# Linear attention and a two-layer FFN in float32: the second stage's up product by Strassen's scheme, with weight sums made early and streamed

## The chip, the cores and the metric

The kernel runs on one core of a Trainium2 chip. The metric is the device time in microseconds (us) of one execution. Three executions of the kernel before took 1128.74, 1130.81 and 1132.51 us; the median, 1130.81 us, is the number to compare with. The profile describes one execution, with the span from its first to its last instruction.

## The reference

Inputs are float32: q, k, v of 8 batches x 8 heads x 576 tokens x 64, a feature matrix w_phi (64 x 128), the FFN weights w_in (512 x 2048) and w_out (2048 x 512), and a slope alpha for each of the 2048 hidden features.

```python
def phi(x):
    proj = np.einsum('bhsd,df->bhsf', x, w_phi)
    proj = proj - np.max(np.abs(proj), axis=-1, keepdims=True)
    return np.concatenate([np.exp(proj), np.exp(-proj)], axis=-1)
q_p, k_p = (phi(q), phi(k))
kv = np.einsum('bhsf,bhsd->bhfd', k_p, v)
z = np.sum(k_p, axis=2)
num = np.einsum('bhsf,bhfd->bhsd', q_p, kv)
den = np.einsum('bhsf,bhf->bhs', q_p, z)[..., None] + 1e-06
x = (num / den)            # 4608 tokens x 512 after a transpose
h = x @ w_in
g = np.maximum(h, 0.0) + alpha * np.minimum(h, 0.0)
return g @ w_out
```

## The kernel before

The whole kernel is one pass with the output transposed (512 features x 4608 tokens). Attention goes by 32 pairs of heads (`attention_units(i)`); the FFN goes by nine chunks of 512 tokens and by sixteen hidden tiles of 128 features. A full-precision product is made of three matmuls on halves: each operand is split into a rounded high half and the remainder, and high x high, low x high and high x low are added in PSUM (`gemm1` for the up product, `gemm2` for the down product). One hidden tile of one chunk takes 4 x 3 matmuls up and 4 x 3 down, each 128 x 128 x 512.

**Two stages.** The first NF1 = 5 hidden tiles make the first stage: their weights stay in SBUF, and their chunks (`ffn1_units`) are woven into attention as soon as the tokens of a chunk are there. Their partial outputs go to `part_d` in DRAM. The other NF2 = 11 tiles make the second stage, after attention: `up2`, `glu2` and `down2` for each chunk and tile, with the weights kept in SBUF, the sum in four PSUM banks (`po`), and at a chunk's end the addition of `part_d` (L745) and the store. The last two first-stage chunks run between the first tiles of the second stage.

**The order.** For everything up to the turn to the second stage the order is written out by hand: each piece of work is put in `todo` with a due time in steps of one attention pair, and the list is sorted; PE, SP, DVE and ACT keep that order. `turn_over` at T2 = 35.4 frees attention's memory and starts the loads of the second stage's weights. In the second stage (`pass2`) only PE's order is fixed; a planner orders the other engines by its own simulation. POOL is never fixed.

**Weights.** They come as 64-bit floats. Each block of 128 x 256 is decoded by `decode_load` (SP, L177), `decode_scale` (ACT, L186), `decode_split` (DVE, L194 to L197), `decode_add` (POOL, L202), `decode_high` (ACT, L137), `decode_low` (POOL, L141) and `decode_store` (SP, L222). There are 20 blocks for the first stage, two to a pair step from the start, and 44 for the second, one every W2D = 0.70 pair steps from W2A = 12.5 on; so some are decoded after the turn. They pass through raw buffers (RW_BUFS = 4), whose store to `w_d` has to end before the buffer takes the next load. WT holds the offsets of a block's steps, from load at -0.70 to store at +0.90.

**Per tile.** `act_g` makes the leaky activation: two ACT reads of PSUM (L251, L252), a join on DVE (L256), the high half on ACT (L137) and the remainder on DVE (L141).

**Lines.** L141 is the helper `low`, a subtraction on the engine that it is given; L137 is a cast on ACT. L335 and L336 subtract a row's largest absolute value on DVE; L358 to L365 (`k_sum`) sum features for z; L487 divides by the denominator on POOL. L527 to L529 are `gemm1`, L534 to L538 `gemm2`. L582 copies a first-stage result from PSUM on ACT. L693 loads a chunk, L728 a partial output, L749 stores an output.

## Time and profile before

| what | value |
|---|---|
| median of three executions | 1130.81 us (1128.74 to 1132.51) |
| the profiled execution, first to last instruction | 1128.8 us |
| its own time beside the span | not listed apart; the shortest execution, 1128.74 us, is as long as the span |
| mean granted TensorE clock | 1.000 |
| attention and seven first-stage chunks | 0 to about 515 us |
| two last first-stage chunks with chunk 0 | about 520 to 600 us |
| second stage alone | from about 600 us on |
| HBM read, written | 93.92 MB, 38.42 MB |

Engines are PE (TensorE matmuls), PEld (its weight loads), DVE, ACT, POOL and SP (which issues most DMAs). A row of a group gives the line, engine and operation, the tiles, the shape and the count, then busy time and mean length (ns) of one, then the idle time before them with what ended it. A row of a table by stage gives the stretch, its length, the busy time of PE, PEld, DVE, ACT and POOL with counts, the granted clock, the share of DMA and GB/s. A row in order of time gives start, length, engine, line and operation. A row of one line's instructions gives shortest/median/longest length in ns.

The page's rows over forty slices of the span:

```profile
DVE  7888958797788777846872332424233423343323
ACT  4777665666666765665553342333333333333331
POOL 1245332332414142253541000000000000000000
```

### The profile page before, as it was taken

What the parts mean: (1) busy time and instruction counts of PE and PEld (TensorE: products, weight loads), DVE (VectorE), ACT (ScalarE), POOL (GpSimd) and SP (SyncE); (2) the same over time, 40 slices, a digit from 0 to 9 for tenths busy, and PEclk for the clock granted to TensorE, in tenths of its full rate; (3) what the DMA queues carried; (4) which work ended last, traced back from release to release, by engine and by line L of the source; (5) the groups of instructions that cost most, each with busy time, mean ns of one, the idle gap of its engine ahead of it and who ended that gap; (6) DMA issues with size and microseconds to landing.
All of it is one profiled execution on the core that took longest, in us unless ns stands there. A gap on an engine that the chain in (4) does not pass through costs nothing.

```text
span 1128.8 us, 18394 instructions
## 1 busy us (share of the span) xinstructions
PE 1114.8 (99%) x7246; PEld 868.3 (77%) x7246; DVE 636.9 (56%) x983; ACT 559.5 (50%) x1148; POOL 212.3 (19%) x217
## 2 busy tenths in 40 slices
PE   8999999999999999999999999999999999999998
PEld 6666777777777777677788888888888888888886
DVE  7888958797788777846872332424233423343323
ACT  4777665666666765665553342333333333333331
POOL 1245332332414142253541000000000000000000
PEclk9999999999999999999999999999999999999999
DMA  5467264546546364466627030303030302020011
GB/s 180 154 185 223 74 202 151 172 155 199 162 155 201 101 212 165 140 211 206 227 81 254 33 106 1 112 1 112 1 112 1 112 1 98 15 93 20 12 64 38
DMA packets 74389, 133.68 MB, mean 118 GB/s; under 512 B 14656, under 2 KB 25024, under 8 KB 73664
## 3 DMA queue, kind: packets, MB, share of 16 engines
q1 hardware_dynamic: 72000, 122.48, 33.7%
q0 software_dynamic: 2016, 9.96, 2.6%
q8 instruction: 57, 0.93, 0.3%
q14 instruction: 28, 0.23, 0.1%
q10 hardware_dynamic: 288, 0.07, 0.0%
HBM read 93.92 MB, written 38.42 MB: 117 GB/s over the span
## 4 chain that ended last, share of the span: by engine, by line
PE 90%; DVE 6%; DMA 2%; ACT 1%; issue 1%; SPq 0%; DVEq 0%; ACTq 0%
PE h L527 11%; PE h L529 11%; PE h L528 11%; PE po L534 8%; PE po L538 8%; PE po L536 8%; PE kv L372 5%; PE pj L331 5%; PE n L437 5%; PE o L534 4%; PE o L538 3%; PE o L536 3%; PE d L455 2%; PE qt L418 2%; DVE m L335 1%; PE kv L389 1%
## 5 line engine op out<-in xcount | busy, mean ns | idle before, releaser
L256 DVE SCALAR_TENSOR_TENSOR g<-r,aln,g 128x512 f32<-128x512 f32 x144 | 111.4, 774 | 312.1 <-ACT g L252 311.6
L251 ACT ACTIVATE r<-h 128x512 f32<-128x512 f32 x143 | 85.9, 601 | 276.3 <-PE h L529 276.1
L141 DVE TENSOR_TENSOR gl<-g,gh 128x512 fp32r<-128x512 f32 x144 | 104.3, 726 | 84.8 <-ACT gh L137 84.6
L137 ACT CAST gh<-g 128x512 fp32r<-128x512 f32 x144 | 90.0, 625 | 97.6 <-DVE g L256 97.5
L252 ACT ACTIVATE g<-h 128x512 f32<-128x512 f32 x144 | 85.8, 596 | 9.8 <-DVE r L249 6.4
L335 DVE TENSOR_REDUCE m<-pj 128x8 f32<-128x1024 f32 (+1 forms) x66 | 78.2, 1184 | 13.8 <-PE pj L331 13.7
L534 PE MATMUL po<-gh,wd 128*128 128x512 f32 x216 | 84.3, 391 | 0.2 <-ACT gh L137 0.2
L536 PE MATMUL po<-gh,wd 128*128 128x512 f32 x216 | 84.3, 390 | 0.0
L538 PE MATMUL po<-gl,wd 128*128 128x512 f32 x216 | 83.9, 390 | 0.0
L202 POOL TENSOR_TENSOR aw<-ew,aw 128x256 f32<-128x256 f32 x64 | 57.5, 899 | 127.5 <-DVE ew L197 126.9
L336 DVE TENSOR_TENSOR t<-pj,m 128x1024 f32<-128x1024 f32 (+1 forms) x66 | 78.7, 1192 | 2.4
L331 PEld LDWEIGHTS pj<-w_sb,raw 64*128 64x128 f32 x1024 | 63.5, 190 | 18.2 <-issue 11.7
L331 PE MATMUL pj<-w_sb,raw 64*128 64x128 f32 x1024 | 72.7, 281 | 4.1 <-DVE t L336 2.5
L534 PE MATMUL o<-gh,w 128*128 128x512 f32 x180 | 76.0, 422 | 0.4 <-ACT gh L137 0.2
L527 PE MATMUL h<-xh,w 128*128 128x512 f32 x180 | 76.0, 422 | 0.0
L487 POOL TENSOR_TENSOR s<-s,rr 128x576 f32<-128x576 f32 x32 | 47.8, 1492 | 142.0 <-DMA rr<-rec_d 107.9
L428 ACT ACTIVATE qf<-qt 128x512 f32<-128x512 f32 x128 | 68.4, 614 | 6.3 <-PE qt L418 6.3
L538 PE MATMUL o<-gl,w 128*128 128x512 f32 x180 | 71.0, 395 | 0.2 <-DVE gl L141 0.2
L534 PE MATMUL po<-gh,w 128*128 128x512 f32 x180 | 70.2, 390 | 0.7 <-ACT gh L137 0.7
L529 PE MATMUL h<-xl,w 128*128 128x512 f32 x180 | 70.7, 393 | 0.0
L536 PE MATMUL o<-gh,w 128*128 128x512 f32 x180 | 70.6, 392 | 0.0
L528 PE MATMUL h<-xh,w 128*128 128x512 f32 x180 | 70.5, 392 | 0.0
(110 smaller groups left out, 2407.7 us busy)
## 6 DMA issues: line engine op xcount, KB each, us to landing
xr<-x_d SPq DMA_DIRECT2D x18, 1024.0 KB
raw<-kq_dram SPq DMA_DIRECT2D x31, 576.0 KB
v<-v_dram SPq DMA_DIRECT2D x32, 320.0 KB
w_d<-raww SPq DMA_DIRECT2D x38, 256.0 KB
rr<-rec_d SPq DMA_DIRECT2D x64, 144.0 KB
x_d<-s SPq DMA_DIRECT2D x32, 288.0 KB
part_d<-os SPq DMA_DIRECT2D x36, 256.0 KB
pt<-part_d SPq DMA_DIRECT2D x9, 1024.0 KB
```

What stands on the lines that cost most here:

```text
L137: return act.copy(dst, src)
L141: return eng.tensor_tensor(dst, src, f(hi), op=ALU.subtract)
L251: act.activation(st["r"], ps, AF.Relu, scale=-1.0)
L256: dve.scalar_tensor_tensor(g, st["r"], aln[:, ff : ff + 1], g, op0=ALU.mult, op1=ALU.add)
L331: pe.matmul(dst[h, j], lhsT=c["raw"][hs, ts], rhs=w_sb[hs], start=True, stop=True)
L335: dve.tensor_reduce(m, src, axis=AX.X, op=ALU.max, apply_absolute_value=True)
L527: pe.matmul(ps, lhsT=wt[0][:, ws], rhs=xh, start=n == 0, stop=False)
L528: pe.matmul(ps, lhsT=wt[1][:, ws], rhs=xh, start=False, stop=False)
L529: pe.matmul(ps, lhsT=wt[0][:, ws], rhs=xl, start=False, stop=n == NK - 1)
L534: pe.matmul(ps, lhsT=wt[2][:, ws], rhs=gh, start=first, stop=False)
L536: pe.matmul(ps, lhsT=wt[3][:, ws], rhs=gh, start=False, stop=False)
L538: pe.matmul(ps, lhsT=wt[2][:, ws], rhs=gl, start=False, stop=last)
```

## The change

The number of first-stage tiles goes from 5 to 4, so the second stage has 12. They are grouped in NU = 6 units of two tiles. Chunk 0 is computed as before. Chunks 1 to 8 are taken as four pairs, and the up product of a unit with a pair of chunks is made as a 2 x 2 block product (two tiles x two halves of the 512 inputs x two chunks) with seven block products in place of eight, in the Strassen-Winograd form. A block product is 2 x 3 matmuls.

- **Weights.** The four weight sums of each unit are made while the weights are decoded (`sum_of`: a sum or difference on POOL, the high half on ACT, the remainder on POOL, a store on SP) and kept in DRAM (`u_d`) with the four plain blocks. Second-stage blocks are decoded every 0.46 pair steps from 10.6 on, so that all are through before the turn. For each pair of chunks, each unit's seven blocks are loaded by SP into one of two buffers (`load_up`). The down weights stay in SBUF.
- **Inputs.** `prepare` loads half the inputs of two chunks, makes four sums on POOL, and splits seven blocks into halves on ACT and DVE.
- **Products.** `unit` issues the seven products. Partial sums that two results share stay in one PSUM bank, to which later products are added; ACT copies them out in between (`copied`), and DVE adds the copies to other banks (`added`). The first chunk's tiles are activated and split at once and their down products (`some_down`, two banks at a time) run between the products of the next unit. The second chunk's activated tiles are kept, and are split and multiplied after the last unit (`second`).
- `load_part` is written where the last tile's sum ends; the special order of the very last tile's matmuls and its DVE activation go.

```diff
-NF1 = 5
+NF1 = 4
 NF2 = NF - NF1
+NU = NF2 // 2
+A11, A12, A22, A21 = range(4, 8)
...
-W2A = 12.5
-W2D = 0.70
+W2A = 10.6
+W2D = 0.46
...
-    w_d = tc.dram_tile([NF2, P, 4, 512], F32, name="w_d")
+    u_d = tc.dram_tile([NU, P, 8, 2, WN], F32, name="u_d")
+    w_d = tc.dram_tile([NF2, P, 2, 512], F32, name="w_d")
...
+    def sum_of(u, n):
+        def make():
+            p, q, op = ((A21, A22, ALU.add), (0, A11, ALU.subtract), (A11, A21, ALU.subtract), (A12, 1, ALU.subtract))[n]
+            a = w1t.tile([P, WN], F32, tag="ws", name=f"ws{u}_{n}", bufs=S2_BUFS + 1)
+            blk4[u, n] = a
+            pool.tensor_tensor(a, blk4[u, p], blk4[u, q], op=op)
+
+        def high():
+            blk4[u, n, 1] = w1t.tile([P, 2, WN], F32R, tag="wo", name=f"wo{u}_{n}", bufs=S2_BUFS)
+            rnd(act, blk4[u, n, 1][:, 0, :], blk4[u, n])
+
+        def rest():
+            t = blk4[u, n, 1]
+            low(pool, t[:, 1, :], blk4[u, n], t[:, 0, :])
+
+        def store():
+            nc.sync.dma_start(u_d[u, :, n], f(blk4[u, n, 1]))
...
+            if k in (1, 2, 3):
+                for m in ((0,), (1, 2), (3,))[k - 1]:
+                    dt = 0.2 * (m == 2)
+                    todo += [(t + dt + SW[e], g) for e, g in enumerate(sum_of(u, m))]
...
+    def load_up(p, u):
+        t = late["wu"].tile([P, 7, 2, WN], F32R, tag="wu", name=f"wu{p}_{u}", bufs=2)
+        if p:
+            nc.sync.dma_start(f(t[:]), u_d[u, :, 0:7])
+        else:
+            pool.dma_start(t[:, 0:4], u_d[u, :, A11:])
+        wu[p, u] = t
...
+    def prepare(p, j):
+        c = 2 * p - 1
+        raw = late["xt"].tile([P, 2, 2 * C2], F32, tag="xr", name=f"xr{p}_{j}", bufs=1)
+        src = x_d.rearrange("(k j) p s -> j p k s", j=2)[j][:, :, c * C2 : (c + 2) * C2]
+        nc.sync.dma_start(raw, src)
+        b11, b12, b21, b22 = (raw[:, k, t * C2 : (t + 1) * C2] for k in range(2) for t in range(2))
+
+        def split(n, src):
+            t = late["xo"].tile([P, 2, C2], F32R, tag=f"x{n}_{j}", name=f"xo{p}_{n}_{j}")
+            rnd(act, t[:, 0], src)
+            low(dve, t[:, 1], src, t[:, 0])
+            xo[p, n, j] = (t[:, 0], t[:, 1])
+
+        t1, t2 = (late["xt"].tile([P, C2], F32, tag=f"t{n}", name=f"t{p}_{n}_{j}") for n in range(2))
+        pool.tensor_tensor(t1, b12, b11, op=ALU.subtract)
+        pool.tensor_tensor(t2, b22, t1, op=ALU.subtract)
+        pool.tensor_tensor(b12, b22, b12, op=ALU.subtract)
...
+        pool.tensor_tensor(b21, b21, t2, op=ALU.subtract)
...
+    def product(ps, p, u, n, first, end):
+        w = wu[p, u][:, n]
+        for j in range(2):
+            wh, wl = (w[:, k, j * P : (j + 1) * P] for k in range(2))
+            xh, xl = xo[p, n, j]
+            pe.matmul(ps, lhsT=wh, rhs=xh, start=first and j == 0, stop=False, skip_group_check=True)
+            pe.matmul(ps, lhsT=wl, rhs=xh, start=False, stop=False, skip_group_check=True)
+            pe.matmul(ps, lhsT=wh, rhs=xl, start=False, stop=end and j == 1, skip_group_check=True)
...
+        product(a, p, u, A11, True, False)
+        p1 = copied(a, f"p1_{tag}")
+        product(b, p, u, A12, True, True)
+        g = g1(f"11_{tag}")
+        added(g, b, p1)
+        leaky(g, g, f1, f"11_{tag}")
+        gq[c1, f1] = halves(g, f"11_{tag}")
+        some_down()
+        product(a, p, u, 1, False, False)
+        u2 = copied(a, f"u2_{tag}")
+        c = bank(1, f"pc{tag}")
+        product(c, p, u, 0, True, False)
+        some_down()
+        product(a, p, u, 2, False, False)
+        u3 = copied(a, f"u3_{tag}")
+        g22 = g2(0), g2(1)
+        added(g22[1], c, u3)
+        some_down()
+        product(a, p, u, A22, False, True)
+        g = g1(f"21_{tag}")
+        leaky(a, g, f2, f"21_{tag}")
+        gq[c1, f2] = halves(g, f"21_{tag}")
+        some_down()
+        product(c, p, u, 3, False, True)
+        added(g22[0], c, u2)
+        leaky(g22[0], g22[0], f1, f"12_{tag}")
+        leaky(g22[1], g22[1], f2, f"22_{tag}")
+        stored[c2, f1], stored[c2, f2] = g22
...
+        for p in range(1, NC2 // 2 + 1):
+            c1, c2 = 2 * p - 1, 2 * p
+            for u in range(NU):
+                if u + 1 < NU:
+                    load_up(p, u + 1)
+                unit(p, u)
+                some_down(len(downs))
+                queue(c1, 2 * u)
+                queue(c1, 2 * u + 1)
+            more_pairs = p < NC2 // 2
+            if more_pairs:
+                load_up(p + 1, 0)
+            for u in range(NU):
+                second(c2, 2 * u)
+                if u == 0 and more_pairs:
+                    prepare(p + 1, 0)
+                some_down(4)
+                second(c2, 2 * u + 1)
+                if u == 2 and more_pairs:
+                    prepare(p + 1, 1)
+        some_down(len(downs))
```

More of the change, by code (lines that the diff above doesn't have):

```diff
@@ L108 @@
 TL = 31.4
-WL = dict(load=-1.20, scale=-0.40, split=0.0, add=0.28, high=0.60, low=0.80, store=0.95)
+WL = dict(load=-0.85, scale=-0.40, split=0.0, add=0.28, high=0.60, low=0.80, store=0.95)
 FS = (0.06, 0.25)
@@ L235, in decode_at @@
         return [(t + (WT if t < TL else WL)[k], lambda u=u: u(*blk, WN)) for k, u in stages.items()]
[L237 removed]
+    inplace = {(ff, z) for ff in range(NF1) for z in range(2)}
     W = {ff: weight_tile(w1p, f"w{ff}")[0] for ff in range(NF1)}
@@ L665, in fused_kernel, with load_down, up_plain, of @@
     pinned = {et.PE, et.SP, et.DVE, et.Activation}
-    w2t = {}
-    late_pools = {}
-    def load_w2(ffs):
+    late, wd = {}, {}
+    def load_down(pool_, ffs):
         for ff in ffs:
-            pool.dma_start(w2t[ff], w_d[ff])
+            t = pool_.tile([P, 2, 512], F32R, name=f"wd{ff}")
+            pool.dma_start(t, w_d[ff])
+            wd[ff] = [t[:, n, :] for n in range(2)]
+    def load_up(p, u):
+        t = late["wu"].tile([P, 7, 2, WN], F32R, tag="wu", name=f"wu{p}_{u}", bufs=2)
+        if p:
+            nc.sync.dma_start(f(t[:]), u_d[u, :, 0:7])
+        else:
+            pool.dma_start(t[:, 0:4], u_d[u, :, A11:])
+        wu[p, u] = t
+    wu = {}
+    def up_plain(ff):
+        u, r = divmod(ff, 2)
+        t = wu[0, u]
+        def of(j):
+            n = ((A11, A12), (A21, A22))[r][j // 2] - A11
+            cs = slice(j % 2 * P, (j % 2 + 1) * P)
+            return t[:, n, 0, cs], t[:, n, 1, cs]
+        return of
     def turn_over():
@@ L800, in fused_kernel @@
-    for ff in range(NA, NF2):
-        for z in range(2):
-            if ff < NA + ND and z == 0:
-                continue
-            half, t = half_tile(w2b if z and ff >= NL2 else w2u, f"w{'ud'[z]}{NF1 + ff}")
-            W[NF1 + ff] = W.get(NF1 + ff, []) + half
-            w2l[ff, z] = t
-    for ff, z in sorted(w2l, key=lambda k: k[0] + 3 * k[1]):
-        pool.dma_start(w2l[ff, z], w_d[slot_d(NF1 + ff), :, 2 * z : 2 * z + 2])
-    load_x(1)
-    with tc.manual_schedule(engines={et.PE}):
-        pass2(seq[NB:])
+    dec.close()
@@ new lines, in fused_kernel, with some_down, copied, leaky @@
+    downs = []
+    def some_down(k=1):
+        for _ in range(k):
+            if downs:
+                downs.pop(0)()
+    def copied(ps, name):
+        t = late["cp"].tile([P, C2], F32, tag="cp", name=name, bufs=3)
+        act.copy(t, ps)
+        return t
+    def leaky(src, g, ff, name):
+        r = late["g"].tile([P, C2], F32, tag="r", name=f"r{name}", bufs=G_BUFS)
+        act.activation(r, src, AF.Relu, scale=-1.0)
+        act.activation(g, src, AF.Relu)
+        dve.scalar_tensor_tensor(g, r, aln[:, NF1 + ff : NF1 + ff + 1], g, op0=ALU.mult, op1=ALU.add)
```

259 lines of the change are left out of this document (141 added, 118 removed).

## The prediction

> **What bounds the kernel now.** I read the page's busy times first, then its chain, then the table by stage that sums each engine's busy time over stretches, and last the order of time on TensorE in a stretch without stops.
>
> ```profile
> span 1128.8 us, 18394 instructions
> PE 1114.8 (99%) x7246; PEld 868.3 (77%) x7246; DVE 636.9 (56%) x983; ACT 559.5 (50%) x1148; POOL 212.3 (19%) x217
> PE 90%; DVE 6%; DMA 2%; ACT 1%; issue 1%; SPq 0%; DVEq 0%; ACTq 0%
> ```
>
> TensorE is busy for 99% of the span and makes 90% of the chain that ended last. The 56% of DVE is an average, though. The stretches below are seven pairs of attention (105 to 229), fourteen pairs (229 to 460), one early and one late pair, the last two pairs, and a piece of the second stage. Columns: length, then PE, PEld, DVE, ACT, POOL with their counts.
>
> ```profile
> 105.00:229.20 124.20, 124.16 (x1019) 91.06 (x1017) 94.96 (x144) 79.81 (x175) 42.98 (x37) 1.00 0.50 153
> 229.20:460.50 231.30, 230.94 (x1946) 168.89 (x1944) 183.72 (x282) 151.44 (x330) 70.31 (x65) 1.00 0.51 164
> 123.00:141.00 18.00, 18.00 (x149) 13.29 (x147) 16.87 (x27) 12.00 (x28) 5.33 (x5) 1.00 0.28 85
> 460.50:477.00 16.50, 15.68 (x129) 11.04 (x127) 15.06 (x24) 9.22 (x21) 4.71 (x4) 1.00 0.50 145
> 477.00:510.00 33.00, 33.00 (x223) 23.27 (x220) 16.08 (x24) 21.59 (x51) 14.61 (x15) 1.00 0.70 228
> 728.00:784.00 56.00, 56.00 (x248) 46.26 (x247) 20.38 (x29) 20.53 (x37) 0.00 (x0) 1.00 0.16 57
> ```
>
> In the second stage DVE works 36% of the time and POOL not at all. In attention a pair takes 231.3/14 = 16.52 us and DVE works 183.72/14 = 13.12 us of it, 79%. TensorE sets the pace, but DVE is close behind: it filled 94% of the stretch from 123 without any stop of TensorE, and 91% of the one from 460.5 with a loss of 0.82 us. So I read two stages with two nearest limits.
>
> What one matmul is worth comes from starts, not from durations. Between these two rows lie 43 matmuls:
>
> ```profile
> 712.24 0.39 PE L527 MATMUL h<-x2hl,w 128*128 128x512 f32 x1
> 721.99 0.39 PE L536 MATMUL po<-gh,w 128*128 128x512 f32 x1
> ```
>
> 9.75/43 = 0.2267 us each. The listed 0.39 us overlaps with the next ones.
>
> **The change, part by part.** *Matmuls.* Before: 9 chunks x 16 tiles x 24 = 3456 of 512 columns. After: the first stage has 4 tiles, 9 x 96 = 864. In the second, chunk 0 has 12 x 24 = 288. Each of the four pairs of chunks has 6 units of 7 products of 6 matmuls (252) in place of 288, and 288 for the down product. The sum is 864 + 288 + 4 x 540 = 3312, so 144 fewer: 144 x 0.2267 = **32.6 us**. They leave unevenly. Seven chunks of the first stage lie in attention and lose 24 each there, 168 x 0.2267 = 38.1 us; the other two lose 10.9 us; the second stage gains 72 (24 in chunk 0, 48 in the pairs), 16.3 us. If TensorE stayed the only limit, the span would be 1128.8 - 32.6 = 1096.2 us.
>
> *Attention.* The middle fourteen pairs hold four pairs per chunk, so 6 matmuls fewer each: 16.52 - 6 x 0.2267 = 15.16 us on TensorE. What DVE has to do in a pair changes in three ways, priced by these groups and, below them, the shortest/median/longest of the same instructions:
>
> ```profile
> L256 DVE SCALAR_TENSOR_TENSOR g<-r,aln,g 128x512 f32<-128x512 f32 x144 | 111.4, 774 | 312.1 <-ACT g L252 311.6
> L141 DVE TENSOR_TENSOR gl<-g,gh 128x512 fp32r<-128x512 f32 x144 | 104.3, 726 | 84.8 <-ACT gh L137 84.6
> L195 DVE SCALAR_TENSOR_TENSOR aw<-raww,aw 128x256 uint32<-128x256 uint32 x64 | 37.6, 588 | 2.2
> L358 DVE TENSOR_TENSOR y<-xk 128x1024 f32<-128x1024 f32 x23 | 31.5, 1371 | 0.0
> L194 DVE TENSOR_SCALAR aw<-aw 128x256 uint32<-128x256 uint32 x64 | 29.2, 456 | 17.3 <-ACT aw L186 12.0 <-POOL xl L141 5.1
> L196 DVE TENSOR_SCALAR ew<-aw 128x256 uint32<-128x256 uint32 x64 | 29.1, 455 | 6.7 <-DVE aw L195 0.5
> L197 DVE SCALAR_TENSOR_TENSOR ew<-raww,ew 128x256 f32<-128x256 uint32 x64 | 29.1, 454 | 2.2
> L362 DVE TENSOR_TENSOR z<-y 128x512 f32<-128x512 f32 x23 | 19.6, 854 | 2.1
> L365 DVE TENSOR_TENSOR z<-z,k 128x512 f32<-128x512 f32 x23 | 19.2, 836 | 3.1 <-ACT k L344 0.8
> ...
> L194 DVE TENSOR_SCALAR aw<-aw x64: 226/290/1392, 15.2 to 588.8; 128x256 uint32<-128x256 uint32 x64
> L195 DVE SCALAR_TENSOR_TENSOR aw<-raww,aw x64: 424/426/1666, 15.5 to 589.6; 128x256 uint32<-128x256 uint32 x64
> L196 DVE TENSOR_SCALAR ew<-aw x64: 293/294/1496, 15.9 to 590.2; 128x256 uint32<-128x256 uint32 x64
> L358 DVE TENSOR_TENSOR y<-xk x23: 1212/1215/2309, 104.4 to 477.2; 128x1024 f32<-128x1024 f32 x23
> L362 DVE TENSOR_TENSOR z<-y x23: 691/693/1966, 105.7 to 478.5; 128x512 f32<-128x512 f32 x23
> L365 DVE TENSOR_TENSOR z<-z,k x23: 691/692/1709, 107.6 to 479.3; 128x512 f32<-128x512 f32 x23
> ```
>
> First, a quarter of a tile per pair goes: 0.25 x (0.774 + 0.726) = -0.38 us. Second, weight blocks come every 0.46 pair steps in place of 0.70 (W2D), 2.17 per pair for 1.43, 0.74 more. At the medians (0.290 + 0.426 + 0.294, and 0.45 for L197) a block is 1.46 us of DVE: +1.08 us. Third, POOL. The same DVE instruction takes 0.290 us mostly and 1.392 us at worst: it is held up by something, and POOL's instructions are what runs beside it.
>
> ```profile
> L202 POOL TENSOR_TENSOR aw<-ew,aw 128x256 f32<-128x256 f32 x64 | 57.5, 899 | 127.5 <-DVE ew L197 126.9
> L141 POOL TENSOR_TENSOR xl<-xr,xh 128x512 fp32r<-128x512 f32 x34 | 45.3, 1340 | 9.0 <-ACT xh L137 8.7
> L141 POOL TENSOR_TENSOR raww<-aw,raww 128x256 fp32r<-128x256 f32 x38 | 32.4, 854 | 82.3 <-ACT raww L137 82.3
> ```
>
> The excess of mean over median is 64 x (0.166 + 0.162 + 0.161) + 23 x (0.156 + 0.161 + 0.144) = 41.9 us, 0.2 us for each of the 217 POOL instructions. A pair gains 0.74 x 2 POOL instructions for blocks and 1.09 x 2 for the weight sums (24 sums for 48 blocks, a difference and a remainder each): 3.65. Their price to DVE lies between nothing (they meet instructions that aren't held) and their own 0.85 us; I take the measured 0.2: +0.73 us.
>
> DVE then has 13.12 - 0.38 + 1.08 + 0.73 = 14.55 us of 15.16, 96%. The two stretches above put what it can fill without stopping TensorE at 91 to 94%; with 93% a pair takes 15.65 us, 0.49 us over TensorE's, 14 x 0.49 = **7 us** lost. The seven pairs before them have room: two chunks' 48 matmuls off 124.2 us leave 113.3 us, and DVE's 94.96 becomes 94.96 - 3.0 + 5 blocks x 1.46 + 24 x 0.2 = 104.1 us, 92%: no loss. The last pairs, at half load, take the rest.
>
> SP issues 2.6 more transfers per pair (0.74 loads, 0.74 stores, 1.09 sums). Blocks have four raw buffers (RW_BUFS), and with 0.46 a load comes 0.24 pair steps, 3.6 us, behind the store that frees its buffer. A load that waits holds what is queued behind it on SP: the reciprocals, their spread to rr, the next raw. Such waits exist already:
>
> ```profile
> SPq L177 <- DMA w_d<-raww: 24.6, 7, 5.9
> ```
>
> They cost between nothing and, at 3.5 us for each of 48 loads, far more than TensorE sees, since the queued transfers are wanted a fraction of a pair later. I take 3 us.
>
> *Second stage.* A unit has 42 matmuls for products and 24 down: 66 x 0.2267 = 15.0 us. Its other work is priced by these rows, with the DVE rows above:
>
> ```profile
> L745 DVE TENSOR_TENSOR pt<-po,pt 128x512 f32<-128x512 f32 x35 | 23.2, 688 | 1.8 <-PE po L538 0.8
> L137 ACT CAST gh<-g 128x512 fp32r<-128x512 f32 x144 | 90.0, 625 | 97.6 <-DVE g L256 97.5
> L251 ACT ACTIVATE r<-h 128x512 f32<-128x512 f32 x143 | 85.9, 601 | 276.3 <-PE h L529 276.1
> L252 ACT ACTIVATE g<-h 128x512 f32<-128x512 f32 x144 | 85.8, 596 | 9.8 <-DVE r L249 6.4 <-DMA part_d<-os 3.3
> L582 ACT COPY os<-o 128x512 f32<-128x512 f32 x36 | 21.0, 594 | 26.3 <-PE o L538 18.5 <-DMA part_d<-os 3.9 <-issue 2.6
> ```
>
> ACT: three copies at 0.594 (the nearest PSUM read), four tiles at 1.197, two casts at 0.625: 7.8 us. DVE: three sums at 0.688, four joins at 0.774, two remainders at 0.726: 6.6 us. Both hide in 15.0 us. The waits that the scheme adds are in bank `a`: TensorE may add the next product only when ACT has copied the last one out. The third copy (u3) has one half-tile of down work before it, 6 x 0.2267 = 1.36 us for a copy of 0.6; behind a waiting product stand all later matmuls. With ACT half idle that fits; one foreign ACT instruction in front still fits by 0.1 us. Below nothing it can't go, since no matmul is saved by a wait. The upper end is two foreign instructions, some 0.6 us a unit, 14 us in 24 units.
>
> The streamed sums are 128 x 14336 B = 1.84 MB a unit, with one buffer ahead, so 15.0 us to land. A chunk change of before moved 3.1 MB, issued here and gone after 721:
>
> ```profile
> 710.81 0.38 SPq L749 DMA_DIRECT2D out_dram<-pt  x1
> ...
> 711.79 1.11 SPq L728 DMA_DIRECT2D pt<-part_d  x1
> ...
> 712.00:722.00 10.00, 10.00 (x46) 8.27 (x45) 4.39 (x7) 5.38 (x10) 0.00 (x0) 1.00 0.89 304
> ```
>
> At 304 GB/s 1.84 MB take 6.1 us: hidden, unless other transfers more than double that. Preparing the next inputs has the 144 down matmuls of the second chunk, 32.6 us: DVE 12 x 0.726 + 14 x 0.69 + 8 x 0.688 = 23.9 us, POOL 8 x 1.34 = 10.7 us, and two inputs of 1 MB one after the other through one buffer. It fits, with the least room of all. I take **5 us** for the whole second stage, between 0 and 14 + 10.
>
> *Sum.* 1128.8 - 32.6 + 7 + 3 + 5 = 1111.2 us. The median of the three runs, 1130.81, lies 2.0 above that span; so I forecast **1113 us**.
>
> **The rivals.** *TensorE stays the only limit*: no loss in attention and in the units, 1096 + 2 = 1098 us. For it: 94% in the stretch from 123 cost nothing. Against: 0.82 us at 91% from 460.5.
>
> *POOL's new instructions pace attention through DVE* (slower). At 0.85 us each a middle pair's DVE time is 13.82 + 3.65 x 0.85 = 16.9 us, at 93% 18.2 us: 3.0 x 14 = 43 us, and the first seven pairs become (99.3 + 24 x 0.85)/0.93 = 128.7 us, 15 us over. That is 1096.2 + 58 + 8 + 2 = 1164 us. It decides from about 0.5 us an instruction, where the loss is some 30 us. For it: single instructions grew by 1.1 us, and both decode and sums crowd the same pairs. Against: the measured mean is 0.2. The Trainium skill, page "SBUF — State Buffer", section "Who interferes with whom", calls the port pair of the two engines an exclusive lock on which the later instruction fully blocks, and spares DVE instructions with at most one SBUF input outside the two-port modes. This rule speaks for whole blocks of POOL's length, so for this rival; the longest rows above agree with it, and the mean row says how seldom it happens so far.
>
> *Copies in the units are late*: 14 us in place of a few, 1127 us; for it, DVE and ACT work in one chain there (sum, two activations, join, cast); against, both are about half idle.
>
> That the matmuls don't go is not a rival: the counts are fixed by the loops.
>
> **How the numbers follow.** Forecast, 1106 to 1122: 0.42. TensorE alone, 1096 to 1106: 0.17. Late copies or inputs, 1122 to 1136: 0.19. POOL and DVE, 1136 to 1170: 0.22. The range reaches from 1099 to 1142 and leaves out most of the last case and the edge of the second. About 0.3% (3.4 us) can be told from no change, so faster is below 1127.4: 0.42 + 0.17 + 0.07 of the third = 0.66; the same, 0.10; slower, 0.02 + 0.22 = 0.24.
>
> **What would show it.** Middle pairs of 15.2 to 16 us with DVE above 90%; decode rows (L194 to L196) not above 0.6 us on average, or else the slower rival; units of 15 to 15.6 us with POOL idle in them; a gap on TensorE at the first product of a pair would be late inputs, one at the A22 product late copies. The forecast is wrong if pairs stay at 16.5 us, or if units take 16 us and more.

## The result, and the profile after

The changed kernel takes **1158.53 us** (median of four executions, 1154.55 to 1159.72); beside it the kernel before took 1130.9 us. The ratio is 1.024, with a 95% interval of 1.0218 to 1.0261: slower, outside the forecast's range of 1099 to 1142. The page of after, with the totals, the chain that ended last, and two rows over forty slices:

```profile
span 1157.1 us, 18486 instructions
PE 1109.3 (96%) x7102; PEld 848.2 (73%) x7102; DVE 727.0 (63%) x1078; ACT 620.8 (54%) x1269; POOL 304.4 (26%) x301
...
DVE  7888888979988898841245444834465435634352
...
PEclk9999999989999999998999999999999999999999
...
PE 48%; DMA 6%; DVE 5%; issue 2%; ACT 2%; POOL 1%; SPq 0%; DVEq 0%; ACTq 0%; POOLq 0%
```

The 144 matmuls are gone (7246 - 7102), and yet TensorE was busy for 1109.3 us, 5.5 less than before. Its share of the last chain fell from 90% to 48%, and two slices show a granted clock below full, where the mean of before was 1.000. Table by stage of after, in the columns of the prediction's: fourteen middle pairs, six units of the first pair of chunks, and the second chunk's pass behind them.

```profile
222.96:465.60 242.64, 224.60 (x1864) 158.57 (x1862) 212.90 (x323) 154.73 (x356) 117.06 (x117) 0.96 0.64 202
641.65:730.80 89.15, 89.15 (x385) 71.97 (x384) 40.90 (x59) 43.55 (x78) 1.68 (x1) 1.00 0.39 143
730.80:767.50 36.70, 36.10 (x159) 29.37 (x158) 23.85 (x30) 15.70 (x28) 10.47 (x7) 1.00 0.47 165
```

**Where 61 us went.** With TensorE alone the span would have been 1096.2 us; it was 1157.1. Three pieces make up the difference:

- *Attention, 35.5 us.* The rows of the numerator's matmuls (first and last start) mark the end of pair 31; the first row is of before, the second, in its own fence, of after.

```profile
L437 PE MATMUL n<-qf,sf x512: 405/406/457, 26.8 to 506.7; 128*64 128x288 f32 x171
```

```profile
L458 PE MATMUL n<-qf,sf x512: 406/406/457, 26.7 to 508.2; 128*64 128x288 f32 x171
```

Ahead of this mark the first stage has 150 matmuls fewer (six chunks of 24, and ten steps of the seventh in place of twelve). So it should have come 150 x 0.2267 = 34.0 us earlier, at 472.7, and came at 508.2. I call the distance from 472.7 a kernel's loss in attention (from 506.7 with five tiles). The expectations speak of the start of pair 31's products, 1.7 us ahead of the mark (506.5 in after).

- *The second stage, 16.2 us.* From the first product at 641.65 to the last down matmul at 1152.97 lie 2184 matmuls, 495.1 us at 0.2267, which took 511.3.
- *The turn between them, the remaining 9.2 us.*

**What a stop in attention looks like.** In order of time near 318 us, start and length: DVE, then ACT, then TensorE.

```profile
306.89 1.22 DVE L356 TENSOR_REDUCE m<-pj 128x8 f32<-128x1024 f32 x1
308.14 1.22 DVE L357 TENSOR_TENSOR t<-pj,m 128x1024 f32<-128x1024 f32 x1
309.28 1.22 DVE L379 TENSOR_TENSOR y<-xk 128x1024 f32<-128x1024 f32 x1
310.60 1.96 DVE L383 TENSOR_TENSOR z<-y 128x512 f32<-128x512 f32 x1
312.66 1.04 DVE L386 TENSOR_TENSOR z<-z,k 128x512 f32<-128x512 f32 x1
...
316.01 0.74 DVE L277 SCALAR_TENSOR_TENSOR g<-r,aln,g 128x512 f32<-128x512 f32 x1
...
316.79 0.62 ACT L137 CAST gh<-g 128x512 fp32r<-128x512 f32 x1 [4.45 <-DVE g L277]
...
320.07 0.58 PE L352 MATMUL pl<-w_sb,raw 64*128 64x128 f32 x1 [1.78 <-ACT qf L449]
```

DVE runs without a pause from 306.9, so the join at L277 comes at 316.0. ACT, in its fixed order, stands at the cast for 4.45 us; the exponentials behind it (L449) free a PSUM bank late, and TensorE stops for 1.8 us. Then the clock falls. The same places by stretches (the value ahead of the last two columns is the granted clock):

```profile
316.50:319.90 3.40, 1.75 (x8) 1.01 (x6) 3.03 (x7) 3.11 (x9) 1.10 (x1) 1.00 0.56 202
319.90:323.30 3.40, 3.23 (x30) 2.80 (x34) 1.92 (x6) 3.40 (x7) 1.61 (x2) 0.50 0.03 1
323.30:326.70 3.40, 3.40 (x40) 1.94 (x34) 2.88 (x7) 2.01 (x5) 0.00 (x0) 1.00 0.47 131
```

Attention has four such stretches at half clock (251.6 for 6.8 us; 319.9, 357.4 and 459.8 for 3.4 each): 17.0 us, so up to 8.5 us lost. TensorE's own waits there, in sum, count and longest:

```profile
PE pl L352 <- ACT qf L449: 8.3, 5, 2.9
PE o L562 <- DVE gl L141: 6.8, 6, 1.7
PE d L476 <- ACT qf L449: 2.4, 2, 1.9
PE pj L352 <- DVE t L357: 2.3, 5, 0.7
```

With the shorter rows they add up to 24.3 us, where the kernel before has 1.0 us. So up to 24.3 - 1.0 + 8.5 = 32 of the 35.5 us are seen.

### The profile page after: what moved, and what is told of

Same layout as the page of the kernel before. It is cut to its first block, busy times and chain, and to the rows that moved or that the text cites. A ratio compares the mean times of both kernels' runs of the same rounds, so it can differ in the third digit from the quotient of the medians.

```text
span 1157.1 us, 18486 instructions
## 1 busy us (share of the span) xinstructions
PE 1109.3 (96%) x7102; PEld 848.2 (73%) x7102; DVE 727.0 (63%) x1078; ACT 620.8 (54%) x1269; POOL 304.4 (26%) x301
## 4 chain that ended last, share of the span: by engine, by line
PE 48%; DMA 6%; DVE 5%; issue 2%; ACT 2%; POOL 1%; SPq 0%; DVEq 0%; ACTq 0%; POOLq 0%
PE po L562 7%; PE po L558 7%; PE po L560 7%; DMA xr<-x_d 4%; PE pa L850 4%; PE pa L849 4%; PE pa L851 4%; DVE xo L141 2%; PE pc L850 2%; PE pc L851 2%; PE pc L849 2%; PE h L550 1%; PE h L548 1%; PE h L549 1%; PE pb L851 1%
## 5 line engine op out<-in xcount | busy, mean ns | idle before, releaser
L562 PE MATMUL po<-gl,wd 128*128 128x512 f32 x432 | 169.6, 393 | 4.1 <-DVE gl L141 4.1
L558 PE MATMUL po<-gh,wd 128*128 128x512 f32 x432 | 170.0, 394 | 0.3 <-ACT gh L137 0.3
L560 PE MATMUL po<-gh,wd 128*128 128x512 f32 x432 | 170.2, 394 | 0.0
L869 DVE SCALAR_TENSOR_TENSOR g<-r,aln,g 128x512 f32<-128x512 f32 x96 | 70.0, 747 | 63.6 <-ACT g L868 63.3
L562 PEld LDWEIGHTS po<-gl,wd 128*128 128x128 f32 x432 | 81.5, 189 | 24.2 <-DVE gl L141 6.2
L558 PEld LDWEIGHTS po<-gh,wd 128*128 128x128 f32 x432 | 81.4, 188 | 19.2 <-ACT gh L137 0.7
L560 PEld LDWEIGHTS po<-gh,wd 128*128 128x128 f32 x432 | 81.5, 189 | 18.2
L839 POOL TENSOR_TENSOR xr<-xr,t 128x512 f32<-128x512 f32 x8 | 13.6, 1698 | 268.7 <-DVE xo L141 268.7
L352 PE MATMUL pj<-w_sb,raw 64*128 64x128 f32 x1024 | 76.9, 287 | 6.8 <-DVE t L357 4.6
L352 PEld LDWEIGHTS pj<-w_sb,raw 64*128 64x128 f32 x1024 | 66.9, 195 | 21.2 <-issue 9.8
L899 DVE TENSOR_TENSOR g<-pc,u 128x512 f32<-128x512 f32 x48 | 33.2, 692 | 76.3 <-ACT u L862 57.4
L277 DVE SCALAR_TENSOR_TENSOR g<-r,aln,g 128x512 f32<-128x512 f32 x48 | 38.6, 805 | 61.7 <-ACT g L273 61.7
L849 PE MATMUL pa<-xo,wu 128*128 128x512 f32 x192 | 76.1, 396 | 0.0
L850 PE MATMUL pa<-xo,wu 128*128 128x512 f32 x192 | 76.0, 396 | 0.0
L851 PE MATMUL pa<-xo,wu 128*128 128x512 f32 x192 | 75.9, 396 | 0.0
L449 ACT ACTIVATE qf<-qt 128x512 f32<-128x512 f32 x128 | 68.8, 615 | 2.2 <-PE qt L439 2.2
```

What stands on the lines that cost most here:

```text
L352: pe.matmul(dst[h, j], lhsT=c["raw"][hs, ts], rhs=w_sb[hs], start=True, stop=True)
L558: pe.matmul(ps, lhsT=wt[0][:, ws], rhs=gh, start=first, stop=False)
L560: pe.matmul(ps, lhsT=wt[1][:, ws], rhs=gh, start=False, stop=False)
L562: pe.matmul(ps, lhsT=wt[0][:, ws], rhs=gl, start=False, stop=last)
L849: pe.matmul(ps, lhsT=wh, rhs=xh, start=first and j == 0, stop=False, skip_group_check=True)
L850: pe.matmul(ps, lhsT=wl, rhs=xh, start=False, stop=False, skip_group_check=True)
```

## The experiments

The texts name these theories. A: DVE's sum of work paces attention. B: POOL's weight sums do. H: the place of one join in the order does. C: four tiles leave TensorE too little work to cover attention's own chain. D: addresses off multiples of 64 bytes slow the units' matmuls. E: operands on different sides of SBUF do. T: the burst of loads makes the stop at the turn. The ratios are to executions of the kernel before beside them, at 1131 to 1132 us. The loss in attention is read from one profiled execution of each kernel. Four kernels whose edits leave attention as it is (e3, e6, e9, e12) lost 34.3, 35.0, 34.9 and 34.1 us there, so a difference of some 1.5 us in the last column says nothing.

| kernel | time, us | ratio to before (95%) | loss in attention |
|---|---|---|---|
| changed kernel | 1158.53 | 1.0218 to 1.0261 | 35.5 |
| e1 slower decode | 1170.02 | 1.0311 to 1.0362 | 21.6 |
| e2 no sums | 1151.18 | 1.0146 to 1.0188 | 31.5 |
| e7 half of the decode off DVE | 1146.58 | 1.0121 to 1.0158 | 28.0 |
| e8 decode spread | 1177.07 | 1.0388 to 1.0423 | 54.0 |
| e10 join early | 1159.92 | 1.0212 to 1.0286 | 31.5 |
| e11 chunks earlier | 1159.23 | 1.0208 to 1.0266 | 45.3 |
| e13 five tiles, fast decode | 1134.94 | 1.0013 to 1.0034 | 6.7 |
| e14 e7 and e10 | 1148.97 | 1.0100 to 1.0198 | 25.8 |
| e15 all of the decode off DVE | 1139.81 | 1.0031 to 1.0097 | 16.4 |
| e16 e15 and e10 | 1138.09 | 1.0030 to 1.0074 | 17.7 |

### Attention: the decode's rate, and the sums

e1 decodes as slowly as the kernel before; two down tiles are then loaded later.

```diff
-W2D = 0.46
+W2D = 0.70
-            load_down(late["wd"], range(4, ND))
+            load_down(late["wd"], range(4, 8))
...
+        load_down(late["wd"], range(8, ND))
```

> Second-stage blocks every 0.70 pair steps as before, from 10.6 on; weight sums with their blocks. Theory A (DVE's fixed queue, filled by the denser decode, holds up the leaky activation, ACT behind it and TensorE): a middle pair falls from 17.3 us to 15.2 to 15.8 us, attention ends 20 to 30 us earlier, 1128 to 1138 us. Rival B (POOL's weight sums block DVE): pairs fall by a third of that, since sums still come, 1148 to 1152 us. Rival C (a first stage with four tiles has too little matmul work per pair to cover the rest, and the clock drops after each stop): pairs stay at 17 us, 1155 to 1160 us.

It gave 14 us back in attention and lost more than that at the turn: from the last numerator matmul to the first product of the pairs it took 156 us, against 133, because the last blocks were decoded there, with ACT waiting in order for loads issued late (29.8 us in sum). The whole is 1170 us, in none of the three ranges. But the run says more than that about A. Its middle stretch:

```profile
222.96:465.60 242.64, 231.78 (x1987) 164.95 (x1983) 196.11 (x296) 156.47 (x351) 91.72 (x94) 0.99 0.57 182
```

With 196.11 us DVE has nearly the work of the kernel before in the same stretch (193.88), and 21.6 us are lost in attention all the same. So neither the fast decode nor more work on DVE is needed for the larger part of the loss.

With W2D = 0.60 and the 32 bytes of e3 together (e5) it was 1171.5, with 28.8 us lost in attention; both of its ranges lay lower. So in this design the fast decode saves time as a whole: it costs less in attention than it spares at the turn.

> Blocks every 0.60 pair steps and the 32 bytes, the two together. Theory A with D: between e1 and the base in attention, pairs of 15.5 to 16.5 us, and 9 us off the units: 1122 to 1135 us. Rival C with D: 1149 us.

e2 leaves the weight sums out:

```diff
-                for m in ((0,), (1, 2), (3,))[k - 1]:
-                    dt = 0.2 * (m == 2)
-                    todo += [(t + dt + SW[e], g) for e, g in enumerate(sum_of(u, m))]
+                pass
```

> Leaves out the weight sums (48 POOL, 24 ACT instructions, 24 stores); the units multiply plain blocks in their place, loaded in two transfers. Decode stays at 0.46. Theory A: DVE keeps 14.7 us or so a pair of 15.2, pairs fall by 0.5 us at most: 1146 to 1153 us. Rival B: pairs fall to 15.5 us, 1128 to 1135 us. Rival C: no change.

Seven us in all, four of them in attention: B falls, which had expected 1128 to 1135. The time lies where A had put it, and C had expected no change.

### Attention: decode work, the order, and the cover

e7 and e14 take the DVE work and the addition of the down blocks out, e15 and e16 that of all second-stage blocks (there the condition is `ff >= NF1` alone).

```diff
 def decode_split(ff, z, o, n):
...
+        if z and ff >= NF1:
+            return
```

> The four DVE instructions and the POOL addition are left out for the 24 down blocks of the second stage, whose values are then wrong; everything else, loads, casts, remainders and stores, stays. Theory A (DVE's load in its fixed order paces attention): DVE falls from 212.9 us to about 185 in the middle stretch, nearly all middle pairs take 15.15 to 15.5 us, pair 31's products start at 478 to 486 instead of 506.5, no stretch of half clock stands in attention, and the time falls by 20 to 28 us less what the turn keeps, to 1130 to 1140. Rival C (with four first-stage tiles TensorE has too little work between attention's parts, whatever DVE does): the pairs keep 16.5 to 17.5 us and the time is above 1150.

The middle stretch of e7:

```profile
222.96:465.60 242.64, 227.68 (x1881) 160.90 (x1880) 182.41 (x262) 156.39 (x359) 104.49 (x103) 0.96 0.63 202
```

A falls as I had put it: DVE did 182.41 us there, less than the 193.88 us of the kernel before in the same stretch, and 28 us were still lost. The 1146.58 us lie above A's range, but also below the 1150 that C had as its least. The next three edits touch only the order: e8 sets the four DVE instructions of a block apart, e10 the join ahead of the projections, e11 the chunks earlier.

```diff
-WT = dict(load=-0.70, scale=-0.25, split=0.0, add=0.15, high=0.42, low=0.55, store=0.90)
+WT = dict(load=-0.70, scale=-0.25, split0=0.0, split1=0.09, split2=0.18, split3=0.27, add=0.32, high=0.50, low=0.62, store=0.92)
```

> Only the order is changed: the four DVE instructions of a second-stage block stand 0.09 of a pair apart, with the later steps moved by 0.02 to 0.17, instead of in one run. Theory A1 (joins and projections wait behind the run of four, the load itself would fit): the long pairs shorten to under 17 us, DVE's share of the middle stretch rises above 90%, pair 31's products start at 485 to 497, the time falls by 8 to 20 us, to 1138 to 1150. Theory A2 (the load of DVE with POOL's hold on it is the limit, the order matters little): pairs stay at 17 us or more and the time is 1152 to 1162.

A clear miss, above both ranges: 18.5 us more were lost in attention. The early pairs, whose first-stage blocks use the same offsets, became longer too (pair 6: 16.9 us in place of 10.3).

```diff
-FG = (0.15, 0.34, 0.52)
+FG = (0.08, 0.34, 0.52)
-GL = (0.20, 0.42, 0.58)
+GL = (0.08, 0.42, 0.58)
-GE = (0.20, 0.30, 0.48)
+GE = (0.08, 0.30, 0.48)
```

> Only the due time of the first stage's join on DVE changes: 0.08 pair steps behind its up product instead of 0.15 (0.20 in the last chunks). With eight steps to a pair two of a chunk's four up products end at 0.905 of a pair, so that the join was due at 1.055, behind the two projections' reductions and subtractions and the feature sums that stand at 1.0 (some 9 us of DVE); now it is due at 0.985, ahead of them. Theory H (the join's place behind that run of DVE, and ACT's cast waiting for it in ACT's fixed order, make most of the stops): the waits of the projections for ACT near 249, 318, 388 and 457 us go, pairs 16, 20, 22 and 28 fall below 17.5 us, pair 31's products start at 485 to 496 instead of 506.5, the time is 1138 to 1149. Theory A (DVE's sum of work with POOL's hold is the limit): DVE is as late elsewhere, pair 31 starts at 502 or later, the time is 1154 to 1160.

The stops that I had traced went, and with them all half clock in attention. Yet only 4.0 us came back, since other waits took their place. TensorE's waits in attention of e10:

```profile
PE pj L352 <- DVE t L357: 12.6, 9, 1.7
PE o L562 <- DVE gl L141: 5.7, 5, 1.6
PE n L458 <- ACT ds L486: 3.1, 3, 1.8
```

Now the second projection waits for the first one's reduction and subtraction (2.3 us before the edit, 12.6 after). The turn was also longer (139.5 us from the mark to the first product of the pairs, against 133.4), so the time didn't move. H is refuted as the main cause.

```diff
-FB = 8.03
+FB = 7.91
-FL = 1.40
+FL = 1.30
```

> All first-stage chunks from the third on start 0.12 pair steps earlier (FB 7.91 instead of 8.03, their input 0.10 earlier in the chunk's own time), so that up products end at 0.285 and 0.785 of a pair and joins are due at 0.435 and 0.935, ahead of the projections. Theory H expects what it does of e10: stops at the joins go, pair 31 starts at 485 to 498, the time is 1138 to 1150; a loss stays possible where the chunk's input arrives later than its new due time. Theory A: 1154 to 1160.

Worse in attention by 9.8 us, of which three more matmuls ahead of the mark make 0.7: one stop of 3.75 us stood at 147, where a down product waited for a partial output's copy.

What was left was C, and whether decode and order hid behind each other.

```diff
-        todo += decode_at(W2A + W2D * n, blk)
+        todo += decode_at(10.6 + 0.46 * n if n < 38 else W2A + W2D * n, blk)
```

> The kernel before with its own five first-stage tiles, 38 of its 44 second-stage blocks decoded every 0.46 pair steps from 10.6 on, as in the changed kernel; the last six, which need memory that the turn frees, stay where they were. No weight sums. Theory C (four tiles leave too little TensorE work to cover attention's chains, so stops come with them; with five the cover holds): attention keeps 16.5 us a pair, pair 31 starts within 5 us of 504.9, the time is 1118 to 1136. Theory A (the rate of decoding makes the stops): pair 31 starts at 515 or later, with stops and half clock as in the changed kernel, and the time is above 1138.

This is the kernel before with the fast decode for 38 of its 44 blocks. Its middle stretch:

```profile
222.96:465.60 242.64, 238.87 (x2007) 173.86 (x2005) 209.17 (x315) 160.38 (x354) 91.12 (x84) 1.00 0.56 175
```

DVE is 86% busy, nearly as in the changed kernel (88%), but with five tiles only 6.7 us are lost and the clock stays full. Pair 31 starts at 511.6, a little later than C had put it (within 5 us of 504.9) and earlier than A (515 or later). The kernel that differs least from this one in all but the tile is e2: the same rate of decoding, no weight sums, four tiles. It loses 31.5 us. So 24.8 us of loss come with the fifth tile's leaving, at an equal rate.

> Both edits together: the DVE instructions and the addition of the 24 down blocks left out, and the join due at 0.08. Theory AH (decode work and the join's place each hide behind the other): pair 31's products start at 474 to 486, more than the 7.6 and 4.0 us that the two gave alone; no half clock in attention. Rival C (four tiles leave TensorE too little work to cover attention's own chain): 494 to 500, about the better of the two alone.

> The four DVE instructions and the addition are left out for all 48 second-stage blocks (values wrong); loads, casts, remainders, sums and stores stay, and the join stays at 0.15. Theory A (decode work on DVE alone): pair 31 at 470 to 480, pairs at 15.15. Theory AH: 486 to 496, since the join still stands behind the projections. Rival C: above 492.

> As e15, with the join due at 0.08. Theory AH and theory A: pair 31 at 468 to 476, pairs at 15.15, stops in attention under 4 us in sum. Rival C: stops of 10 us or more stay, above 482, though DVE is then under 70% busy in the middle stretch.

The middle stretch of e15 and, behind it, TensorE's waits in its attention:

```profile
222.96:465.60 242.64, 229.03 (x1963) 161.86 (x1962) 157.93 (x211) 164.06 (x376) 94.53 (x93) 1.00 0.65 211
...
PE n L462 <- DVE t L361: 4.4, 4, 3.5
PE pj L356 <- DVE t L361: 3.3, 6, 0.7
PE pl L356 <- ACT qf L453: 2.9, 3, 1.7
PE o L562 <- ACT gh L137: 2.5, 3, 1.3
```

DVE is at 65% and TensorE still stops, longest behind the subtraction that follows the projections (L361 on DVE). e14 and e16 came out as C said, and not as the mixed theory AH; e15 came out where AH put it, a little better than C. So taking the decode's work away helps (19 us), and without it the join's place is worth nothing. Together: five tiles with the fast decode lose 6.7 us, four tiles without decode on DVE 16.4, both together 35.5, which is 12.4 more than the two losses added. Neither e13 nor e15 has half clock in attention, so up to 8.5 of these 12.4 us are the half clock that only the combination brings. Which edge of the order makes the 16.4 us was not taken apart further. Nor does a run show that it is the fifth tile's matmuls that were missing, and not something else that comes with four tiles: nearly all offsets of the order by hand were kept from five tiles, and GB gives four buffers in place of five. A run with other matmuls in the fifth tile's place would tell.

### The units' matmuls

In the units nothing stops, but the matmuls stand further apart. TensorE in order of time, the first matmul and the last one of bank a in a pair's six units of after, 383 matmuls apart:

```profile
641.65 0.40 PE L849 MATMUL pa<-xo,wu 128*128 128x512 f32 x1
...
730.76 0.40 PE L851 MATMUL pa<-xo,wu 128*128 128x512 f32 x1
```

89.11/383 = 0.2327 us, against the forecast's 0.2267. All four pairs have this number. e3 shifts the right-hand tiles by 32 bytes.

```diff
+    pad = ctx.enter_context(tc.tile_pool(name="pad", bufs=1, side="right"))
+    pool.memset(pad.tile([P, 8], F32, name="pad32"), 0.0)
```

> 32 bytes are reserved at the top of SBUF's right side, so that every tile there starts at a multiple of 64 bytes like those on the left. Theory D (a matmul whose moving operand and weights stand differently within 64 bytes starts its successor 6.6 ns later): in the units the starts come 0.2268 us apart in place of 0.2327, 24 x 66 x 0.0059 = 9 us less, 1149 us. Rival (the units' pace comes from ACT and DVE at work on the same banks, or from the transfers): 0.2327 stays, 1155 to 1160 us.

0.2323 us and 1159.5 us: D falls. The kernel's pools put tiles at one of two ends of SBUF: side="right" is called the upper end here, all else the lower. Sorted so, the slow matmuls are those whose input block lies at the upper end and whose weights lie at the lower (the product's), or the other way round (down tiles 10 and 11). e6 takes the weights from down tiles in the upper part.

```diff
-        w = wu[p, u][:, n]
+        w = wd[10 + n % 2]
```

> Weights of the seven products (chunks 1 to 8) are taken from the down tiles 10 and 11, which lie high in SBUF, as do the input blocks; the unit's own blocks are still loaded, and not read. The output is not the reference's. Theory E (a matmul whose weights and moving operand lie on different sides of SBUF starts its successor some 6.5 ns later): the matmuls of the units stand 227 to 228.5 ns apart instead of 232.7, a pair's six units take 1.5 to 2.2 us less, and the time falls by 6 to 9 us, to 1149 to 1153. Rival F (the pitch comes from PSUM groups held open, from the engines reading PSUM, or from the stream of weights over the DMA): the pitch stays 232 to 233 and the time 1157 to 1160.

Between two up matmuls the mean of 908 distances fell from 233.4 ns to 228.4, and the time to 1147.62 us, a little more than expected. e12 does it properly: up weights of the pairs beside the inputs at the upper end, all else at the lower.

```diff
-        t = late["wu"].tile([P, 7, 2, WN], F32R, tag="wu", name=f"wu{p}_{u}", bufs=2)
+        n = 7 if p else 4
+        t = late["wu2" if p else "wu"].tile([P, n, 2, WN], F32R, tag="wu", name=f"wu{p}_{u}", bufs=2)
...
+    late["wu2"] = ctx.enter_context(tc.tile_pool(name="wu2", bufs=2, side="right", reuse_waits="tile"))
+    late["xt"] = ctx.enter_context(tc.tile_pool(name="xt", bufs=1, reuse_waits="tile"))
```

> A version that computes everything: the pairs' up weights lie high in SBUF beside the input blocks, and all down weights, activations, copies and partial outputs lie low. Theory E (operands on one side): units' matmuls 227 to 228.5 us/1000 apart instead of 232.7, a pair's six units 87.2 to 87.6 us instead of 89.1, the second pass of a pair some 0.5 us shorter, attention unchanged; time 1146 to 1152. If the pitch in e6 fell for another reason (no reader of the streamed weights), it stays near 232 and the time near 1158.

The same two places of e12, in order of time, again 383 matmuls apart:

```profile
643.27 0.39 PE L850 MATMUL pa<-xo,wu 128*128 128x512 f32 x1
...
731.03 0.40 PE L852 MATMUL pa<-xo,wu 128*128 128x512 f32 x1
```

87.76/383 = 0.2291 us (228.2 ns between up matmuls). The kernel takes 1154.25 us, ratio 1.015 to 1.021. E holds for the distance, and since e12 reads the streamed weights as the changed kernel does, their stream isn't its cause. The time missed its range of 1146 to 1152: four pairs times 1.35 us are 5.4 us, and the medians lie 4.3 us apart. The rest of e6's gain came from stops that were shorter in its profile; the half clock before the last pair, for one, is absent there, but also in e3, which changed nothing at that place.

### The turn, and a joint version

The longest stop of the turn is 5.4 us at 528.9, where ACT's copy of L606 waits for the store of a partial output; 6.8 us at half clock follow. The wait of ACT in after, and in another view the stretch behind the stop:

```profile
ACT os L606 <- DMA part_d<-os: 9.6, 1, 9.6
```

```profile
531.50:538.30 6.80, 4.03 (x10) 3.16 (x11) 1.44 (x2) 2.29 (x4) 3.52 (x5) 0.50 0.70 204
```

e9 parts the burst of 4 MB of weight loads:

```diff
             load_up(0, 0)
             load_down(late["wd"], range(2))
-            load_up(0, 1)
-            load_down(late["wd"], range(2, 4))
...
+            todo.append((t + 0.001, lambda ff=ff: rest_of(ff)))
```

> At the turn 2 MB of weights are loaded first; the next 1 MB follows the first second-stage tile's last up matmul and another 1 MB the second tile's. Theory T (the burst of 4 MB holds up the small transfers at the turn, among them the store of a partial output for which the copy of L606 waits): the stop of 5.4 us near 529 falls below 2.5 us, the 6.8 us of half clock behind it go or halve, and the time falls by 4 to 10 us, to 1148 to 1154. Rival: the small transfers wait for the decoded blocks' own stores and the chain from the last division, and the time stays within 3 us of 1158.5.

1158.81 us, and the stop is 5.3 us: T falls. e17 joins what had helped: e12, e10, and more buffers for the partial outputs.

```diff
-            cur["o", m] = g1p.tile([P, C2], F32, tag="g", name=f"os1_{c}_{m}", bufs=3)
+            cur["o", m] = g1p.tile([P, C2], F32, tag="g", name=f"os1_{c}_{m}", bufs=5)
```

> A version that computes everything: operands on one side as in e12, the join due at 0.08 as in e10, and five buffers in place of three for the first stage's joined tiles and partial outputs, so that the copy of L606 need not wait for a store. Expected from e12 (1154.3), from e10's 4 us in attention and its lack of half clock, and from a turn without the stop of 5 to 6.5 us: 1141 to 1149, still slower than the kernel before. If the turn's length is set by the loads instead, 1150 to 1155.

1153.96 us (ratio 1.0172 to 1.0224), no better than e12 alone; 1141 to 1149 had been expected. In attention 35.3 us were lost, so the 4 us of e10 did not come again, and 6.8 us of half clock stood at 261. ACT's and TensorE's longest waits of e17 from 505 to 540:

```profile
ACT ds L486 <- DMA d<-ds: 7.9, 1, 7.9
...
PE o L558 <- ACT g L273: 5.0, 1, 5.0
```

The wait for the partial output shrank to 0.9 us; one for the transfer of the last pairs' denominators took its place, and TensorE again stopped for 5.0 us. Every one of these transfers goes through SP's fixed queue. What would shorten the turn stays open.

## Why the prediction was wrong

- **Matmuls.** Right in number: 144 fewer. Undisturbed middle pairs (15, 18, 19 and 27) take 15.15 us by their numerators' starts; the forecast was 15.16.
- **Attention, the step that failed.** I took 7 us in the middle pairs: DVE at 14.55 us of work a pair, which it could fill to 93%. They lost 242.64 - 14 x 15.16 = 30.4 us. The row of the middle stretch gives 212.90/14 = 15.2 us of work, 88% filled, and 17.3 us a pair. For the seven pairs ahead I took no loss, with DVE at 92% of 113.3 us; they took 118.56 us, some 5 us more, with DVE at 85%. The work was mis-sized by 0.7 us, but the error is in the model. It asked only whether DVE's sum fits into TensorE's time. e15 has 149.38/14 = 10.7 us of DVE work a pair (in its own fourteen middle pairs, of 16.5 us each) and loses 16.4 us; e1 has the DVE work of the kernel before and loses 21.6; e13 has DVE 86% busy and loses 6.7. So the loss goes with the number of tiles more than with DVE's share. My reading of it, which the waits fit but no run isolates: the fifth tile's matmuls had covered the waits of attention's chain (projection, reduction, subtraction, next projection; join, cast, exponentials), and the change took that cover away and put more work into the chain's engines at once. My evidence for 93%, two stretches of the kernel before, had been measured with the fifth tile in place.
- **The clock.** No term of the sum stood for it. The Trainium skill, page "TensorE: Matmul & The Clock Gate", section "Part 1: The HAM clock gate (the "warmup" mystery)", gives the window as some 3.4 us and half clock as the idle state; the stretches of 3.4 and 6.8 us agree. Its advice to avoid gaps above about 3 us (section "Why this matters for your kernels") is too lenient for this trace: the stop near 318 was 1.8 us, and in the 3.41 us ahead of that half clock TensorE was still busy for 1.79.
- **The price of a POOL instruction** was right, so the slower rival is not what happened, although the time falls into its range. The decode and feature-sum groups of after:

```profile
L192 DVE SCALAR_TENSOR_TENSOR aw<-raww,aw 128x256 uint32<-128x256 uint32 x64 | 40.6, 634 | 2.2
...
L193 DVE TENSOR_SCALAR ew<-aw 128x256 uint32<-128x256 uint32 x64 | 31.9, 499 | 6.6
L379 DVE TENSOR_TENSOR y<-xk 128x1024 f32<-128x1024 f32 x23 | 31.5, 1371 | 0.0
L191 DVE TENSOR_SCALAR aw<-aw 128x256 uint32<-128x256 uint32 x64 | 27.3, 426 | 13.5 <-ACT aw L180 13.5
L383 DVE TENSOR_TENSOR z<-y 128x512 f32<-128x512 f32 x23 | 24.4, 1061 | 2.1
L386 DVE TENSOR_TENSOR z<-z,k 128x512 f32<-128x512 f32 x23 | 21.1, 920 | 2.4
```

By the prediction's own way of counting, with its medians, the excess is 64 x (0.136 + 0.208 + 0.205) + 23 x (0.156 + 0.368 + 0.228) = 52.4 us, 0.17 for each of 301 POOL instructions; the rival needed 0.5. The three decode rows average 0.52 us, below the 0.6 that was to speak for it.
- **SP, 3 us.** No wait of TensorE in attention names a transfer. SP's loads did wait 66 us in sum for the stores that free their buffers, as feared, but ACT and DVE waited only 5.2 us for transfers there. At the turn SP's queue does hold others up; the 9.2 us there were in no term.
- **Second stage.** I took 5 us, for late copies and inputs. Late copies didn't occur: the units run without a stop (PE 89.15 of 89.15 us), so that rival falls too. In their place came the distance of the matmuls, 4 x (89.11 - 383 x 0.2267) = 9.1 us. Inputs were the least room of all, as said; before the last pair the stop was 2.6 us, with 3.4 us at half clock behind it. POOL, DVE and TensorE there, in order of time:

```profile
997.47 1.29 POOL L832 TENSOR_TENSOR t<-xr 128x512 f32<-128x512 f32 x1 [20.57 <-DMA xr<-x_d]
998.84 1.62 POOL L833 TENSOR_TENSOR t<-xr,t 128x512 f32<-128x512 f32 x1
1000.42 1.74 POOL L834 TENSOR_TENSOR xr<-xr 128x512 f32<-128x512 f32 x1
...
998.01 4.70 DVE L141 TENSOR_TENSOR xo<-xr,xo 128x512 fp32r<-128x512 f32 x3 [2.98 <-ACT xo L137]
1002.63 1.74 DVE L141 TENSOR_TENSOR xo<-t,xo 128x512 fp32r<-128x512 f32 x1
1004.30 0.68 DVE L141 TENSOR_TENSOR gl<-g,gh 128x512 fp32r<-128x512 f32 x1
...
1005.03 0.50 PE L562 MATMUL po<-gl,wd 128*128 128x512 f32 x1 [2.55 <-DVE gl L141]
```

Three remainders on DVE took 4.70 us and a fourth 1.74 beside POOL's subtractions; the next, beside none, took 0.68. The remainder that TensorE wanted stood behind them. Here the port rule that I had weighed in attention showed itself: the Trainium skill, page "SBUF — State Buffer", section "Who interferes with whom", lets a DVE instruction with two SBUF inputs contend with a POOL instruction that reads SBUF. The trace agrees, with 1.6 to 1.7 us in place of 0.7.

## What to carry to other kernels

Work that is taken off the bounding engine may also have been the cover of the other engines' chains; before counting it as gain, look at what is left between the two ends of each chain, since shares measured under the old cover don't tell what is reached without it. Removing one stop in a fixed order mostly brings out the next (e10, e17), so the stops need to be counted per chain, not per engine. A stop of TensorE costs more than its length where the clock falls behind it.

## What the hardware showed that I had not expected

- Half clock after short stops: stretches of 3.4 or 6.8 us at a granted clock of 0.5, behind stops of 1.8, 2.6 and 5.4 us. Not behind all: none followed one of 1.9 us at 424.9. The starts of the stretches tell why: from the first at 251.6 on, the next five lie 20, 11, 30, 21 and 139 times 3.413 us apart, so they start on a fixed grid. In the 3.41 us ahead of each, TensorE was busy for 0.66 to 1.85 us. The stop at 424.9 lay across a grid line at 425.7, and TensorE was busy for 2.58 and 2.38 us in the two windows. So what counts here is the share of a grid window and not the length of a stop. No sharp limit shows: a window at 142.4 with 1.84 us had no half clock behind it.
- Up matmuls with input and weights on different ends of SBUF stood 233.4 ns apart, with both at the upper end 228.4 (e6) and 228.2 (e12); in the kernel before, with both at the lower end, 227.1 (767 distances).
- One remainder on DVE took 0.68 us alone and 1.74 us beside POOL's subtractions.
